# Reordering the front of a fused attention and MLP kernel: first tile's keys and queries first, fewer memsets, memory rows copied on chip, the g product behind the first scores

## Chip, cores and metric

The kernel runs on one core of one Trainium2 chip. The metric is the device time of one execution in microseconds (us). Several executions are timed and the median is quoted. "Fast" runs are those within 1.5% of the fastest run of the same kernel. One execution is also profiled. All times inside an execution are from the start of its span.

## The reference, cut to what matters

Chunked attention is followed by a layer norm and a two-layer MLP with a residual. There are 4 batches of 768 tokens, 8 heads of 64, and d_model is 512.

```python
for c in range(24):                       # chunks of 32 queries
    k_ctx = k[:, :, max(0, 32*c-16) : min(768, 32*c+40)]
    k_full = concat([mem_k, k_ctx]); v_full = concat([mem_v, v_ctx])     # 8 memory rows
    a = softmax(q_c @ k_full.T / 8); out_c = a @ v_full
x  = out.transpose(0, 2, 1, 3).reshape(4, 768, 512)
xn = (x - mean(x)) / sqrt(var(x) + 1e-6) * g_ln
return x + maximum(xn @ w_ch1, 0) @ w_ch2        # 512 -> 2048 -> 512
```

## The kernel before

The work goes by tiles of 128 tokens, and three tiles make a unit (eight units in all). In a unit, `up` runs 16 chunks of 128 hidden columns over the tiles' 384 tokens, then `down` runs three times 16 products. The attention of the next unit is threaded between these. Each engine runs its own list of instructions in order. The front of the program, before the first `up`, has nothing to hide behind, and this change is about it.

```python
def stay_busy(n, p=None):                 # dummies: keep TensorE's clock up (L362-366)
    p = slot("mm") if p is None else p
    for _ in range(n):
        nc.tensor.matmul(out=p, lhsT=busy[:, 0:128], rhs=busy, start=True, stop=True)

def scores(b, t): ...   # L281: 8 matmuls KT x QZ into an att buffer, two exponentials on ScalarE into AT
def values(b, t): ...   # L303: 16 matmuls AT x V into an att buffer
def norm(t, xi): ...    # L315: VectorE; divides by the sums, subtracts the mean, times g_row -> xn
def turn_x(...): ...    # L347: 4 transposes of xn on TensorE, a copy on ScalarE -> xT
def up(u, n, hc, t0=0, on_act=False): ...   # L370: 4 matmuls w1c x xT, then a ReLU into rT
# [cut] first memsets and small loads; then
for h in (0, 4):
    for which in range(2):
        load_kq(0, which, 0, CUT[which], h, h + 4)   # k, q of heads 0-3, then k, q of heads 4-7
make_identity(nc, identity)
stay_busy(10)
clear_v(0, nc.vector, lambda: clear_q(0, 0))         # memsets of V's ones and of QZ, VectorE
clear_q(0, 1); clear_k(0); mem_keys(); mem_cols(0)
stay_busy(4)
v_mem(0)                                             # DMA: memory rows of values into V
for g in range(6): load_v_group(0, g)
# [cut] masks on GpSimd; loads of W1 (load_w1), rest of k and q, W2
banks = [slot("mm")[:, :] for j in range(4)]         # four PSUM banks
first_k = [as16(p) for p in banks]                   # turned keys, pair of heads j in bank j
first = slot("att")
first_q = [as16(first[:, i, :]) for i in range(2)] + first_k[0:2]   # queries j=2,3 share banks 0,1
# [cut] transposes and copies of k, q for j = 0..3
nc.tensor.matmul(out=banks[2], lhsT=ones32, rhs=g_one, start=True, stop=True)   # g to 128 rows
nc.vector.tensor_copy(out=g_row, in_=banks[2])
scores(0, 0); scores(0, 1); stay_busy(3)
values(0, 0); norm(0, 0);   stay_busy(3)
scores(0, 2); values(0, 1); norm(1, 1); stay_busy(1)
turn_x(0, 0, 0, "mm");      stay_busy(3)
values(0, 2); norm(2, 2)
for hc in range(3): up(0, 1, hc, 0, True)            # tile 0 alone
turn_x(0, 1, 1); up(0, 1, 3, 0, True); stay_busy(2)
for hc in range(4): up(0, 2, hc, 1, True)            # tile 1
turn_x(0, 2, 2)
for hc in range(4, 8): up(0, 2, hc)                  # tiles 0 and 1
for hc in range(8): up(0, 3, hc, 2)                  # tile 2
# unit 0 goes on with chunks 8-15 at steps 8-15; beside them:
at(7, clear_q, 1, 0); at(9, clear_q, 1, 1); at(10, clear_k, 1)   # QZ, KT of batch 1
at(15, kq_block, 0, j, 6, NG, ...)                               # "K transposes", tiles 3-5
```

The softmax here doesn't subtract the row's maximum and nothing guards it: scores larger than these inputs give would overflow.

## Time and profile before

| | before |
|---|---|
| time, median of 4 runs beside the changed kernel | 218.57 us (218.41 to 218.89) |
| span of the profiled run | 216.0 us |
| first scores (tile 0) | 12.35 us |
| first values (tile 0) | 14.39 us |
| first `up` | 18.28 us |
| chunk 8 of unit 0 | 24.68 us |
| first K transposes of `kq_block` | 30.71 us |
| last matmul | 212.18 us |

The lines that carry the argument are shown in the prediction below.

### The profile page before, as it was taken

How to read it: one execution, taken by the hardware profiler on the slowest of the kernel's cores; microseconds unless marked ns; L12 is line 12 of the kernel's file. 1: busy time of each engine (PE TensorE's matmuls, PEld its weight loads, DVE VectorE, ACT ScalarE, POOL GpSimd, SP SyncE). 2: the span in 40 equal slices, each digit the busy share in tenths (PEclk: the TensorE clock that was granted, in tenths of full speed). 3: DMA queues.
4: the chain of work that ended last, by engine and by line, in shares of the span. 5: the costliest groups of instructions: out<-in, count | busy, mean ns of one | idle time of the engine just before them, and what ended most of it. 6: DMA issues, size and time to landing. Idle time of an engine off the chain costs nothing.

```text
span 216.0 us, 5059 instructions
## 1 busy us (share of the span) xinstructions
PE 210.2 (97%) x2011; PEld 129.8 (60%) x2011; DVE 118.6 (55%) x274; ACT 99.7 (46%) x206; POOL 104.4 (48%) x185
## 2 busy tenths in 40 slices
PE   7999989999999999999999999999999999999993
PEld 2557866557765577546754676456754675466562
DVE  6967675685737548524375349224484447634222
ACT  4478437855893677302653167103761275314100
POOL 7993245699996318974004998507145000400000
PEclk9999999999999999999999999999999999999998
DMA  5999999999999989996312999997674101330012
GB/s 78 182 150 207 209 208 181 200 206 226 148 140 172 102 135 146 151 146 171 48 27 80 142 186 148 138 156 103 176 150 132 49 3 24 91 108 0 0 49 100
DMA packets 87714, 27.37 MB, mean 127 GB/s; under 512 B 78297, under 2 KB 84185, under 8 KB 87642
## 3 DMA queue, kind: packets, MB, share of 16 engines
q0 software_dynamic: 62128, 14.38, 78.2%
q1 hardware_dynamic: 25562, 12.66, 28.2%
q8 instruction: 16, 0.26, 0.5%
q14 instruction: 8, 0.07, 0.1%
HBM read 28.84 MB, written 6.29 MB: 163 GB/s over the span
## 4 chain that ended last, share of the span: by engine, by line
PE 94%; DVE 3%; ACT 1%; issue 1%; ACTq 0%
PE mm L377 37%; PE mm L394 37%; PE att L289 5%; PE att L309 3%; PE mm L366 3%; PE att L179 2%; PE mm L412 2%; PE mm L179 1%; DVE QZ L436 1%; ACT AT L296 1%; PE att L352 1%; PE att L366 1%; DVE rT L385 1%; PE mm L539 0%; DVE xn L329 0%
## 5 line engine op out<-in xcount | busy, mean ns | idle before, releaser
L377 PE MATMUL mm<-xT,w1c 128*128 128x384 f16 (+2 forms) x560 | 89.0, 313 | 0.6 <-DVE rT L385 0.6
L394 PE MATMUL mm<-w2c,rT 128*128 128x512 f16 x368 | 84.4, 379 | 0.0
L377 PEld LDWEIGHTS <-w1c 128*128 128x128 f16 x560 | 58.8, 114 | 23.6 <-issue 1.0
L383 ACT ACTIVATE rT<-mm 128x384 f16<-128x384 f32 (+2 forms) x74 | 33.1, 453 | 72.4 <-PE mm L377 50.2
L394 PEld LDWEIGHTS <-rT 128*128 128x128 f16 x368 | 34.7, 98 | 37.5
L385 DVE TENSOR_SCALAR rT<-mm 128x384 f16<-128x384 f32 (+2 forms) x66 | 34.9, 533 | 33.6 <-PE mm L377 33.5
L401 DVE SCALAR_TENSOR_TENSOR osb<-mm,rstd,xs 128x512 f32<-128x512 f32 x23 | 17.3, 750 | 41.8 <-PE mm L394 24.9
L296 ACT ACTIVATE AT<-att,band 104x512 f16<-104x512 f32 x48 | 30.2, 683 | 9.6 <-PE att L289 8.2
L338 POOL TENSOR_SCALAR veps<-squares 128x1 f32<-128x1 f32 x24 | 4.8, 200 | 42.7 <-ACT junk L335 41.3
L117 POOL DMA_DIRECT2D V<-in_v_dram x24 | 18.4, 772 | 11.0 <-DMA w1c<-in_moe_w_ch_dram 7.8
L335 ACT ACTIVATE junk<-xs,nmean 128x512 f16<-128x512 f32 x24 | 17.3, 721 | 7.1 <-DVE nmean L326 6.7
L329 DVE SCALAR_TENSOR_TENSOR xn<-xs,nmean,g_row 128x512 f16<-128x512 f32 x24 | 18.8, 782 | 0.9
L320 DVE SCALAR_TENSOR_TENSOR xs<-att,rec 128x512 f32<-128x512 f32 x24 | 16.6, 691 | 0.8
L289 PEld LDWEIGHTS <-KT 128*128 128x128 f16 x192 | 12.6, 98 | 4.6 <-issue 1.0
L277 POOL COPY QZ<-kraw 64x768 f16<-64x768 f16 x16 | 13.2, 826 | 3.9 <-DMA kraw<-qraw 3.4
L342 POOL TENSOR_TENSOR rstd<-veps,mhalf 128x1 f32<-128x1 f32 x24 | 13.7, 571 | 2.0
L289 PE MATMUL att<-QZ,KT 128*128 128x128 f16 x192 | 14.6, 219 | 0.0
L269 POOL COPY KT<-KT 128x128 f16<-128x128 f16 (+4 forms) x16 | 4.2, 292 | 18.2 <-DMA KT<-kraw 18.1
L123 POOL DMA_DIRECT2D V<-in_v_dram x16 | 12.0, 791 | 0.9 <-PE mm L377 0.7
L309 PEld LDWEIGHTS <-AT 104*64 104x64 f16 x384 | 7.5, 111 | 6.5 <-ACT AT L296 2.1
L242 POOL DMA_DIRECT2D qraw<-in_q_dram x12 | 11.3, 938 | 0.0
L242 POOL DMA_DIRECT2D kraw<-in_k_dram x12 | 11.2, 934 | 0.0
(76 smaller groups left out, 136.6 us busy)
## 6 DMA issues: line engine op xcount, KB each, us to landing
out_dram<-osb SPq DMA_DIRECT2D x23, 256.0 KB, 2.3
V<-in_v_dram POOLq DMA_DIRECT2D x36, 96.0 KB, 6.9
w1c<-in_moe_w_ch_dram POOLq DMA_DIRECT2D x4, 512.0 KB, 9.6
w2c<-in_moe_w_ch_dram POOLq DMA_DIRECT2D x4, 512.0 KB, 13.5
kraw<-in_k_dram POOLq DMA_DIRECT2D x12, 128.0 KB, 5.3
qraw<-in_q_dram POOLq DMA_DIRECT2D x12, 128.0 KB, 5.4
qraw<-in_q_dram POOLq DMA_DIRECT2D x3, 384.0 KB, 11.6
kraw<-in_k_dram POOLq DMA_DIRECT2D x3, 256.0 KB, 5.7
```

The source lines that it names most:

```text
L117: nc.gpsimd.dma_start(out=V[b % 2][r : r + hi - lo, g, :, 0:64], in_=dram(v, b * H * HS + lo * D, [[64, hi - lo], [HS, H], [1, 64]]),)
L242: nc.gpsimd.dma_start(out=free(dst, 512 * t, [[64, H], [1, 64]]), in_=dram(src, b * H * HS + 128 * t * D, [[D, 128], [HS, H], [1, 64]]),)
L289: nc.tensor.matmul(out=p[:, gg, 128 * j : 128 * j + 128], lhsT=KT[b % 2][:, (4 * g + j) * KW : (4 * g + j) * KW + 128], rhs=QZ[b % 2][:, g ...
L296: nc.scalar.activation(out=free(a, 32 * c, [[512, 2], [64, 8], [1, 32]], KR), in_=free(p, 32 * c, [[512, 2], [64, 8], [1, 32]], KR), func= ...
L320: nc.vector.scalar_tensor_tensor(out=x.rearrange("p (h d) -> p h d", h=H), in0=free(p, 0, [[128, H], [1, 64]]), scalar=1.0, in1=free(r, 0, ...
L329: nc.vector.scalar_tensor_tensor(out=xn[i], in0=x, scalar=nmean[i], in1=g_row, op0=ALU.add, op1=ALU.mult,)
L335: nc.scalar.activation(out=junk, in_=xs[xi], func=ACTF.Square, bias=nmean[i], accum_out=squares[i],)
L377: nc.tensor.matmul(out=p, lhsT=free(w, i, [[4, 128]]), rhs=xT[u % 2][:, dt, lo:hi], start=(dt == 0), stop=(dt == 3),)
L383: nc.scalar.activation(out=o, in_=p, func=ACTF.Relu)
L385: nc.vector.tensor_scalar(out=o, in0=p, scalar1=0.0, scalar2=None, op0=ALU.max)
L394: nc.tensor.matmul(out=p, lhsT=rT[hc][:, 128 * i : 128 * i + 128], rhs=w2c[hc // 4][:, hc % 4, :], start=(hc == 0), stop=(hc == 15),)
L401: nc.vector.scalar_tensor_tensor(out=o, in0=p, scalar=rstd[t % 9], in1=xs[t % 9], op0=ALU.mult, op1=ALU.add,)
```

## The change

The intent is to reach the first scores sooner. The first tile's groups of keys and queries are evicted before the others. About half of the early memsets are shrunk, moved to ScalarE or put off. The memory rows of V are copied on chip instead of loaded by DMA. The product that spreads g over 128 partitions is issued behind the first scores. With it come a new order of tiles 1 and 2 and a first `up` over two tiles.

```diff
+    def keep_mem(b, g0, g1, copy):          # memv16 -> V[96:104, g0:g1], on an engine
@@ clears
-        eng.memset(V[i][:, :, :, 64:HD], 1.0)
+        eng.memset(V[i].bitcast(FP32)[:, :, :, 32:end], TWO_ONES)     # end = 33 at first
@@ loads
-    for h in (0, 4):
-        for which in range(2):
-            load_kq(0, which, 0, CUT[which], h, h + 4)
+    for which in range(2):
+        load_kq(0, which, 0, CUT[which], 0, 4)
     keep(counts...); make_identity(nc, identity)
+    for which in range(2):
+        load_kq(0, which, 0, CUT[which], 4, H)
+    nc.scalar.copy(out=QZ[0][0:64, 0:6, :, 1, :], in_=<zeros of busy>)
-    clear_v(0, nc.vector, lambda: clear_q(0, 0))
-    clear_q(0, 1)
-    clear_k(0)
+    clear_v(0, nc.vector, lambda: (clear_q(0, 0, 0, 6), clear_k(0)), 33)
-    stay_busy(4)
-    v_mem(0)
-    for g in range(6):
+    for g in range(3):
         load_v_group(0, g)
@@ behind the masks on GpSimd, ahead of W1
+    for g in range(3, 6):
+        load_v_group(0, g)
@@ [cut] K, Q copies of groups 0-1 first; keep_mem(0, 0, 6, vec); then
-    nc.tensor.matmul(out=banks[2], lhsT=ones32, rhs=g_one, start=True, stop=True)
-    nc.vector.tensor_copy(out=g_row, in_=banks[2])
     scores(0, 0)
-    scores(0, 1)
-    stay_busy(3)
+    for j in range(2, 4):
+        for par in range(2):
+            keep_q(on[j], first_q[j], 0, j, par, CUT[1], 2, 6)    # j=2 on ScalarE
+    for i in range(2):
+        nc.tensor.matmul(out=banks[i][:, 256:512], lhsT=ones32, rhs=g_one[:, 256*i : 256*i+256], ...)
+        vec(out=g_row[:, 256*i : 256*i+256], in_=banks[i][:, 256:512])
     values(0, 0); norm(0, 0)
+    stay_busy(1); scores(0, 1); stay_busy(4); values(0, 1); norm(1, 1); scores(0, 2)
+    turn_x(0, 0, 0, "mm"); stay_busy(3); values(0, 2); norm(2, 2); turn_x(0, 1, 1, "mm"); stay_busy(2)
+    # up: chunks 0-3 over tiles 0 and 1, then tile 2; chunks 4-7 over all three
@@ unit 0
-            at(7, clear_q, 1, 0); at(9, clear_q, 1, 1); at(10, clear_k, 1)
+            at(8 + par, clear_q, 0, par, 6, NG)         # par = 0, 1: other half of QZ, batch 0
+            at(11, keep_mem, 0, 6, NG, vec)
+            at(13, <memset of V's other ones>); at(14, <memset of memv16's ones>)
@@ unit 1
+            at(1, clear_q, 1, 0); at(2, clear_q, 1, 1); at(3, clear_k, 1)
```

The lines `values(0, 0)` to `up` are condensed here.

More of the change, by code (lines that the diff above doesn't have):

```diff
@@ L45 @@
     memk16 = sb.tile([128, 2, 64], FP16, name="memk16")
-    memv16 = sb.tile([72, B, H, HD], FP16, name="memv16")[64:72, :, :, :]
-    memv32 = sb.tile([72, 512], FP32, name="memv32")[64:72, :]
+    memv16 = sb.tile([104, B, H, HD], FP16, name="memv16")[96:104, :, :, :]
+    memv32 = sb.tile([104, 512], FP32, name="memv32")[96:104, :]
     memKT = sb.tile([128, B * 4, 8], FP16, name="memKT")
@@ L139, in v_mem @@
                         ap=[list(src.ap[0]), [0, NG], [1, H * HD]]),
+        )
+    def keep_mem(b, g0, g1, copy):
+        src = memv16[:, b, :, 0:64]
+        copy(
+            out=V[b % 2][96:104, g0:g1, :, 0:64],
+            in_=bass.AP(tensor=src.tensor, offset=src.offset,
+                        ap=[list(src.ap[0]), [0, g1 - g0], [HD, H], [1, 64]]),
         )
@@ L432, in clear_k, with clear_q, clear_v @@
         nc.vector.memset(KT[i][:, end : end + 32], 0.0)
-    def clear_q(i, par):
-        nc.vector.memset(QZ[i][64 - 64 * par : 128 - 64 * par, :, :, par, :], 0.0)
-    def clear_v(i, eng, between=lambda: None):
+    def clear_q(i, par, g0=0, g1=NG, eng=nc.vector):
+        eng.memset(QZ[i][64 - 64 * par : 128 - 64 * par, g0:g1, :, par, :], 0.0)
+    TWO_ONES = (2.0 ** -7) * (1 + 15 * 2.0 ** -13)
+    def clear_v(i, eng, between=lambda: None, end=HD // 2):
         eng.memset(V[i][0:32, 0, :, 0:64], 0.0)
         eng.memset(V[i][64:96, NG - 1, :, 0:64], 0.0)
-        eng.memset(V[i][:, :, :, 64:HD], 1.0)
+        eng.memset(V[i].bitcast(FP32)[:, :, :, 32:end], TWO_ONES)
         between()
-        for c, g in enumerate((0, NG - 1)):
+        for c, g, rows in ((0, 0, slice(0, 32)), (1, NG - 1, slice(64, 96))):
             eng.tensor_copy(
-                out=free(V[i][:, g, 0, 64:65], 0, [[HD, H]]),
-                in_=free(counts[:, c : c + 1], 0, [[0, H]]),
+                out=free(V[i][rows, g, 0, 64:65], 0, [[HD, H]]),
+                in_=free(counts[rows, c : c + 1], 0, [[0, H]]),
             )
@@ L462 @@
     nc.vector.memset(mhalf, -0.5)
-    nc.vector.memset(memv16[:, :, :, 64:HD], 1.0)
     nc.sync.dma_start(out=memk32, in_=dram(mem_k, 0, [[64, 128], [128 * 64, 2], [1, 64]]))
@@ L472 @@
     make_identity(nc, identity)
+    for which in range(2):
+        load_kq(0, which, 0, CUT[which], 4, H)
     nc.scalar.copy(out=memk16, in_=memk32)
+    nc.scalar.copy(out=QZ[0][0:64, 0:6, :, 1, :], in_=free(busy[0:64, :], 0, [[0, 6], [0, 4], [1, 64]]))
     nc.scalar.copy(out=memv16[:, 0, :, 0:64], in_=memv32.rearrange("p (h d) -> p h d", h=H))
     stay_busy(10)
-    clear_v(0, nc.vector, lambda: clear_q(0, 0))
-    clear_q(0, 1)
-    clear_k(0)
+    clear_v(0, nc.vector, lambda: (clear_q(0, 0, 0, 6), clear_k(0)), 33)
     mem_keys()
     mem_cols(0)
-    stay_busy(4)
-    v_mem(0)
-    for g in range(6):
+    for g in range(3):
         load_v_group(0, g)
@@ L520 @@
         turn_kq(first_k[j], k16[0], j, CUT[0])
+    stay_busy(2, spare)
     for j in range(2):
@@ L526 @@
             keep_q(act, first_q[j], 0, j, par, CUT[1], 0, 6)
+    keep_mem(0, 0, 6, vec)
     stay_busy(3, spare)
@@ L529 @@
         turn_kq(first_k[j], k16[0], j, CUT[0])
-    for j in range(2, 4):
-        keep_k(first_k[j], 0, j, CUT[0], 0, 7, act if j == 2 else vec)
-    stay_busy(4, spare)
+    stay_busy(2, spare)
     for j in range(2, 4):
         turn_kq(first_q[j], q16[0], j, CUT[1])
-    for g0, g1 in ((0, 2), (2, 6)):
-        for j in range(2, 4):
-            for par in range(2):
-                keep_q(act if j == 2 else vec, first_q[j], 0, j, par, CUT[1], g0, g1)
-    nc.tensor.matmul(out=banks[2], lhsT=ones32, rhs=g_one, start=True, stop=True)
-    nc.vector.tensor_copy(out=g_row, in_=banks[2])
-    scores(0, 0)
-    scores(0, 1)
-    stay_busy(3)
+    on = {2: act, 3: vec}
+    for j in range(2, 4):
+        keep_k(first_k[j], 0, j, CUT[0], 0, 2, on[j])
+    for j in range(2, 4):
+        for par in range(2):
+            keep_q(on[j], first_q[j], 0, j, par, CUT[1], 0, 2)
+    for j in range(2, 4):
+        keep_k(first_k[j], 0, j, CUT[0], 2, 7, on[j])
+    stay_busy(3, spare)
+    scores(0, 0)
+    for j in range(2, 4):
+        for par in range(2):
+            keep_q(on[j], first_q[j], 0, j, par, CUT[1], 2, 6)
+    for i in range(2):
+        nc.tensor.matmul(
+            out=banks[i][:, 256:512], lhsT=ones32, rhs=g_one[:, 256 * i : 256 * i + 256],
+            start=True, stop=True,
+        )
+        vec(out=g_row[:, 256 * i : 256 * i + 256], in_=banks[i][:, 256:512])
     values(0, 0)
     norm(0, 0)
-    stay_busy(3)
-    scores(0, 2)
+    stay_busy(1)
+    scores(0, 1)
+    stay_busy(4)
     values(0, 1)
     norm(1, 1)
-    stay_busy(1)
+    scores(0, 2)
     turn_x(0, 0, 0, "mm")
@@ L554 @@
     norm(2, 2)
-    for hc in range(3):
-        up(0, 1, hc, 0, True)
-    turn_x(0, 1, 1)
-    up(0, 1, 3, 0, True)
+    turn_x(0, 1, 1, "mm")
     stay_busy(2)
+    for hc in range(2):
+        up(0, 2, hc)
+    turn_x(0, 2, 2, "mm")
+    for hc in range(2, 4):
+        up(0, 2, hc)
     for hc in range(4):
-        up(0, 2, hc, 1, True)
-    turn_x(0, 2, 2)
+        up(0, 3, hc, 2)
     for hc in range(4, 8):
-        up(0, 2, hc)
-    for hc in range(8):
-        up(0, 3, hc, 2)
+        up(0, 3, hc)
     units = [[t, t + 1, t + 2] for t in range(0, 6 * B, 3)]
@@ L599 @@
         if u == 0:
-            at(7, clear_q, 1, 0)
-            at(9, clear_q, 1, 1)
-            at(10, clear_k, 1)
+            for par in range(2):
+                at(8 + par, clear_q, 0, par, 6, NG)
+            at(11, keep_mem, 0, 6, NG, vec)
+            at(13, nc.vector.memset, V[0].bitcast(FP32)[:, :, :, 33 : HD // 2], TWO_ONES)
+            at(14, nc.vector.memset, memv16[:, :, :, 64:HD], 1.0)
             at(23, clear_v, 1, nc.gpsimd)
@@ L617 @@
         elif u == 1:
+            at(1, clear_q, 1, 0)
+            at(2, clear_q, 1, 1)
+            at(3, clear_k, 1)
             for j in (0, 2):
```

## The prediction

> **What bounds the kernel now.** I read the busy shares first, then the chain of work that ended last, then that chain cut to the first 45 us, then the timeline of that stretch. The first two are one line each of the page:
>
> ```profile
> PE 210.2 (97%) x2011; PEld 129.8 (60%) x2011; DVE 118.6 (55%) x274; ACT 99.7 (46%) x206; POOL 104.4 (48%) x185
> ...
> PE 94%; DVE 3%; ACT 1%; issue 1%; ACTq 0%
> ```
>
> TensorE (PE) is busy for 97% of the span and owns 94% of the last chain. From 50 to 200 us the table by stretches gives PE 149.97 of 150 us. So whatever is late at 50 us is late at the end: the change is worth exactly what it does to PE in the front, where PE is busy partly with dummies (`stay_busy`, L366). The chain in order of time, cut to the front:
>
> ```profile
> 1.25 4.45 PE mm L366 x10
> ...
> 10.75 0.62 PE mm L179 x32
> 11.37 1.05 PE mm L539 x2
> 12.42 0.57 PE att L289 x8
> ...
> 13.07 1.85 ACT AT L296 x3
> ...
> 18.34 0.79 PE mm L377 x12
> ...
> 25.32 1.34 DVE QZ L436
> ...
> 27.51 1.34 DVE QZ L436
> ```
>
> Columns: start, length, engine and line. The first scores (L289) stand behind the g product (L539, 1.05 us); then come the exponentials (L296); the first useful MLP matmuls (L377) start at 18.3 us. Two clears of QZ for the next batch (L436) sit in the chain at 25.3 and 27.5 us: they delay VectorE's (DVE's) evictions, and PE lost 0.7 us (0.55 of it noted as idle on an eviction) before it went on at 29.31. These are the two things that the change attacks. The timeline of the front has the durations that I use below:
>
> ```profile
> 1.48 0.48 DVE L463 MEMSET memv<- 8x512 f16 x1
> 3.08 1.34 DVE L442 MEMSET V<- 128x1536 f16 x1 [0.38 <-issue]
> 6.52 0.87 SPq L136 DMA_DIRECT2D V<-memv  x1
> 8.73 0.26 DVE L169 COPY KT<-memKT 128x384 f16<-128x384 f16 x1
> 11.16 1.30 ACT L204 COPY QZ<-mm 64x128 f16<-64x128 f16 x4
> 14.39 0.44 PE L309 MATMUL att<-V,AT 104*64 104x65 f16 x16 [0.32 <-ACT AT L296]
> ```
>
> That ACT line is two copies of 64x128 (0.26 each) and two of 64x256 (0.37 each).
>
> **What the Trainium skill says.** (1) "VectorE: DVE Perf Modes", section "Zero memsets can be issued as uint32 (trn2)": a memset takes one cycle per element whatever its type. The trace agrees if the 0.38 us of idle noted ahead of each large one is counted: 1.34 + 0.38 = 1.72 us for 1536 elements. So half of the elements is about 0.85 us, and writing the ones as fp32 pairs halves them too. (2) Same page, section "The perf-mode tier table (the rule you actually need)": a 16-bit copy from SBUF to SBUF can run at four elements per cycle. The only such copy here took 0.26 us (0.40 at worst) for 384 elements, which fits. (3) "SBUF — State Buffer", section "Who interferes with whom": such a copy takes a port pair that GpSimd needs too, and one blocks the other. The spread 0.26 to 0.40 may be that; no run shows it yet. (4) "TensorE: Matmul & The Clock Gate", section "The HAM clock gate (the "warmup" mystery)": the array runs at half clock until it has been busy for some microseconds, and again after an idle window. The dummies show the first half: starts 0.427 us apart at first, 0.216 us from about 6.7 us on.
>
> **The change part by part.**
>
> *Before the first scores.* Four dummies go (1.34 us at half clock). The clears of V and QZ that DVE did before 8.0 us shrink: V ones 1.72 to about 0.16 us, QZ 2 x 1.7 to 0.85, the other half going to ScalarE (ACT). GpSimd makes the identity between the two pairs of k/q loads. The first k load landed at 1.31 + 4.2 = 5.5 us, the first q near 7.05, the second k at 8.44, the second q near 9.5; these come out of one queue that is full from 4 us on, so I leave them. New PE order: k turned at 6.1, q at 7.1, second k at 8.45, second q at 9.5 to 10.0. Copies of the first two groups (0.24 latency + 2 x 0.26) end near 10.7, as do three dummies; scores of tile 0 run 10.65 to 11.1, against 12.35 to 12.95. Gain here: 1.7 us.
>
> *The g product behind the scores.* In the built program the new g matmul (now L561) carries a wait on ACT, and counting ACT's increments it is the last QZ copy out of the same bank (heads j=2, groups 2 to 6). The two touch different columns, but the wait is there. In ACT's order those copies come after both exponentials of tile 0. So: scores end 11.1; exponentials 11.35 to 12.6 (1.27 as now); two copies 0.72, to 13.3; g product 1.05, to 14.4; only then, being in order on PE, the values of tile 0, at 14.4. They start at 14.39 now. **The whole 1.7 us is handed back**, and PE stands idle from 11.1 to 13.3.
>
> *Tiles 1 and 2.* Now both scores are issued before the first values and exponentials 0 and 1 run back to back (four in 2.42 us). In the new order scores(1) follow values(0) and one dummy: 14.95 to 15.4; exponentials 15.6 to 16.9 (now 14.23 to 15.49); values(1) 16.95; scores(2) to 17.7; exponentials 17.95 to 19.2 (now to 17.45); values(2) 19.25; the transpose and copy of tile 1 end at 20.65. The first `up`, which needs two tiles now, starts at 20.7 (one tile at 18.27 now). From there: 4 x 0.436 (256 columns) + 0.22 (turn) + 0.2 (tile 2's xn, DVE, near 21.75) + 4 x 0.22 + 4 x 0.65 = 5.65 us, so chunk 8 starts at 26.35 against 24.65: **+1.7 us**.
>
> *Chunks 8 to 15.* PE needs 8 x 0.65 = 5.2 us. Now it took from 24.65 to 30.70, the stall and small gaps within: about 0.8 is saved. But DVE has there 4 evictions x 0.56, two half clears (1.7), the second copy of mem rows (1.0 by the tier table), the ones of V (672 elements, 0.76) and of memv16 (0.5): 6.2 us. It ends 0.9 late, and the K and Q copies for tile 3 queue behind it, so scores(3) wait about that long. Saved 0.8, lost 0.9: **total +1.8**.
>
> *Unit 1.* Both full clears of QZ (1.7 each) and the K clears (0.7) move to its first steps, where DVE evicts every second chunk (0.56 of every 1.31 us). Four PSUM slots cover about two chunks; I count **+0.6**, like the 0.7 seen now. The DMA for mem rows of batch 0 goes (120 KB, hidden; the loads behind it may come 0.6 us earlier), but W1's first chunk lands at 17.8 us (10.83 + 7.0) and is then needed only at 20.7.
>
> Sum: 1.7 - 0.8 + 0.9 + 0.6 = +2.4 us, so 218.6 + 2.4 = 221.0. Laying out the old program's front with the same durations and waits comes within 0.3 us of its trace.
>
> **The rivals.** *As intended:* the g product runs under exponential 0. Then values(0) start near 12.7; but tile 1's copies still stand behind exponential 0, and its scores behind those: I get `up` at about 19.2 and 219.4 in all. For it speaks that 256 columns of each bank are free; against it, the wait in the program. *DMA as the floor:* even a perfect front can't pass W1's first chunk at 17.8 (17.2 without the mem rows' DMA), with the next every 2.55 us. From there, two tiles' chunks back to back reach chunk 8 at 22.9, and without stall the end is some 2.5 us earlier: 216.1. So faster by over 2% (214.3) is all but excluded. *The clock falls back:* 2.2 us of PE idle in a row, with no dummies to fill it, could bring half clock; the front waits on others for the most part, so perhaps 1 to 2 us more: 222.5. *The copy of mem rows is slow:* at one element per cycle it is 3.2 us instead of 1.0, ahead of tile 0's last copies and again in chunks 8 to 15: some 3 us more, 224. The 0.26 us copy speaks against it, the port that it shares with GpSimd for some of it.
>
> **Range and chances.** 221.0 us. The layout's own error is about 0.7 us; the copy and the clock push upwards, the intended case downwards. Range 219.0 to 223.0 for 8 in 10. Slower by over 2% is above 223.0: chance 0.12, from the last two rivals. Faster: 0.02. Within 2%: 0.86.
>
> **What would show it.** Right: scores of tile 0 before 11.5 us; the g product not before 13 and PE idle ahead of it, released by ACT's QZ copy; values(0) within 0.5 us of 14.4; the first L386 (`up`) after 20 us; no stall in chunks 8 to 15 but one before scores(3); one near the clears in unit 1. Wrong: a g product right behind the scores, a copy of mem rows well over 1.2 us, 512-column dummies 0.43 us apart after 11 us, or PE waiting for W1.

## More of the kernel before

For the comparison that follows, here is the table by stretches of 2 us of the front. Its columns are the stretch, its length, then busy us (and instructions) of TensorE (PE), its weight loads (PEld), VectorE (DVE), ScalarE (ACT) and GpSimd (POOL), then the granted TensorE clock (PEclk, 1.00 is full), the DMA share and GB/s.

```profile
12.00:14.00 2.00, 2.00 (x20) 1.10 (x19) 1.54 (x4) 1.37 (x4) 1.89 (x4) 1.00 3.02 132
14.00:16.00 2.00, 1.68 (x28) 1.07 (x27) 0.99 (x4) 1.49 (x3) 1.96 (x4) 1.00 1.32 201
16.00:18.00 2.00, 1.92 (x33) 0.97 (x32) 1.86 (x7) 1.75 (x3) 0.35 (x1) 1.00 1.24 206
```

TensorE is almost never idle here, and the clock column reads 1.00.

## The result, and the profile after

The changed kernel took 220.97 us (median of 4 runs, 220.08 to 221.73) against 218.57 us. The ratio is 1.0106 (95% interval 1.0058 to 1.0155), which is within 2%. A ratio is the mean time of one kernel's fast runs over the mean of the other's fast runs in the same rounds, so it isn't quite the ratio of the medians.

The page of the changed kernel gives the busy shares, and the last chain by engine:

```profile
PE 210.5 (96%) x1978; PEld 129.6 (59%) x1978; DVE 119.9 (55%) x280; ACT 100.1 (46%) x200; POOL 105.4 (48%) x185
...
PE 86%; DVE 6%; DMA 2%; ACT 2%; issue 1%; POOL 1%; POOLq 0%; DVEq 0%; ACTq 0%
```

TensorE is busy as long as before (210.5 to 210.2 us) with fewer dummies, and it owns 86% of the last chain instead of 94%. The chain in order of time shows who took the rest (start, length, engine and line):

```profile
3.63 4.84 DMA kraw<-in_k_dram
...
11.11 0.46 PE att L298 x8
...
11.66 1.26 ACT AT L305 x2
12.92 0.25 ACT QZ L213
13.18 0.38 ACT QZ L213
...
13.60 1.13 PE mm L561 x4
14.73 0.37 PE att L318 x16
15.10 0.32 PE mm L375
15.42 0.70 PE att L298 x8
16.12 1.71 PE mm L375 x4
...
22.00 1.03 PE mm L386 x8
...
31.27 0.96 DVE V L145
...
38.09 0.44 PE att L298 x5
```

The scores (L298) end near 11.6. Two exponentials follow on ScalarE, then its two QZ copies, and only then the g product (L561) and the values (L318). Four dummies at 16.12 take 1.71 us. Later, VectorE's work of chunks 8 to 15 is on the chain until scores(3), at 38.09. The timeline names the wait and the sizes:

```profile
7.96 0.98 DVE L145 COPY V<-memv 8x3072 f16<-8x3072 f16 x1
8.09 0.90 POOL L502 TENSOR_TENSOR zero<-zero 128x1 f32<-128x1 f32 x1
9.07 0.19 POOL L503 TENSOR_TENSOR band<-band,zero 128x1 f32<-128x1 f32 x1
13.60 1.13 PE L561 MATMUL mm<-g_one,ones 1*128 1x256 f32 x4 [2.04 <-ACT QZ L213]
15.92 1.91 PE L375 MATMUL mm<-busy 128*128 128x512 f16 x4
19.05 0.80 POOL L117 DMA_DIRECT2D V<-in_v_dram  x1 [2.19 <-DMA w1c<-in_moe_w_ch_dram]
```

The bracket at L561 says that TensorE was idle for 2.04 us until ScalarE's copy of QZ. The table by stretches shows what came of it:

```profile
12.00:14.00 2.00, 0.40 (x2) 0.37 (x3) 0.41 (x1) 1.54 (x4) 2.00 (x4) 1.00 1.71 106
14.00:16.00 2.00, 2.00 (x30) 1.48 (x29) 1.63 (x4) 0.00 (x0) 2.00 (x4) 0.86 1.04 148
16.00:18.00 2.00, 2.00 (x16) 0.60 (x13) 0.99 (x4) 1.27 (x2) 0.86 (x2) 0.50 1.22 194
18.00:20.00 2.00, 2.00 (x31) 1.39 (x25) 1.44 (x5) 0.77 (x2) 0.80 (x1) 0.78 1.24 202
```

TensorE is idle for 1.6 of the 2 us from 12 to 14. From about 15.5 to 18.9 us its clock is halved. It looks 100% busy there and does half of the work.

To see where the time went, I cut each trace at five landmarks: first scores, chunk 8 of unit 0, first K transposes, the first `down` product after scores(3) (the ninth of unit 0), last matmul. The lengths in between add up to the last matmul:

| us | first scores | to chunk 8 | to K transposes | past scores(3) | to last matmul | sum |
|---|---|---|---|---|---|---|
| before | 12.35 | 12.32 | 6.03 | 5.03 | 176.45 | 212.18 |
| after | 10.95 | 16.66 | 5.29 | 5.46 | 176.53 | 214.90 |
| difference | -1.40 | +4.34 | -0.74 | +0.43 | +0.08 | +2.72 |

Everything is decided before 38 us. The stretch from the first scores to chunk 8 grew by 4.34 us, and that is what had to be explained.

The four runs of the changed kernel also have a mean granted clock each: 0.992 in the two at 220.08 and 220.34 us, 0.984 in the two at 221.59 and 221.73 us. One stretch of 3.4 us at half clock lowers the mean of a 218 us span by 0.5 x 3.4 / 218 = 0.008. So the slower pair fits two such stretches, or one of twice the length. That is worked out, not seen: only one run has a trace.

### The profile page after: what moved, and what is told of

It reads as the page before. It is cut to its first block, busy times and chain, and to the rows that moved or that the text cites. A ratio compares the mean times of both kernels' runs of the same rounds, so it can differ in the third digit from the quotient of the medians.

```text
span 218.4 us, 4984 instructions
## 1 busy us (share of the span) xinstructions
PE 210.5 (96%) x1978; PEld 129.6 (59%) x1978; DVE 119.9 (55%) x280; ACT 100.1 (46%) x200; POOL 105.4 (48%) x185
## 4 chain that ended last, share of the span: by engine, by line
PE 86%; DVE 6%; DMA 2%; ACT 2%; issue 1%; POOL 1%; POOLq 0%; DVEq 0%; ACTq 0%
PE mm L403 36%; PE mm L386 35%; PE att L298 5%; PE att L318 4%; DMA kraw<-in_k_dram 2%; PE mm L421 2%; PE att L188 1%; DVE rT L394 1%; ACT AT L305 1%; DVE KT L203 1%; PE mm L375 1%; DVE xn L338 1%; DVE xs L329 1%; DVE QZ L445 1%; PE att L361 1%
## 5 line engine op out<-in xcount | busy, mean ns | idle before, releaser
L386 PEld LDWEIGHTS <-w1c 128*128 128x128 f16 x528 | 57.8, 114 | 23.9 <-issue 0.5
L392 ACT ACTIVATE rT<-mm 128x384 f16<-128x384 f32 (+2 forms) x66 | 31.7, 481 | 72.5 <-PE mm L386 51.1
L394 DVE TENSOR_SCALAR rT<-mm 128x384 f16<-128x384 f32 (+2 forms) x66 | 35.4, 540 | 32.5 <-PE mm L386 32.3
L286 POOL COPY QZ<-kraw 64x768 f16<-64x768 f16 x16 | 14.0, 878 | 3.6 <-DMA kraw<-qraw 3.0
L298 PEld LDWEIGHTS <-KT 128*128 128x128 f16 x192 | 13.1, 100 | 4.3 <-issue 0.4
L298 PE MATMUL att<-QZ,KT 128*128 128x128 f16 x192 | 15.4, 223 | 0.3 <-DVE QZ L213 0.3
L351 POOL TENSOR_TENSOR rstd<-veps,mhalf 128x1 f32<-128x1 f32 x24 | 13.3, 553 | 2.0
L318 PEld LDWEIGHTS <-AT 104*64 104x64 f16 x384 | 7.7, 112 | 7.3 <-ACT AT L305 2.7
```

Source lines behind the costliest of these rows:

```text
L298: nc.tensor.matmul(out=p[:, gg, 128 * j : 128 * j + 128], lhsT=KT[b % 2][:, (4 * g + j) * KW : (4 * g + j) * KW + 128], rhs=QZ[b % 2][:, g ...
L386: nc.tensor.matmul(out=p, lhsT=free(w, i, [[4, 128]]), rhs=xT[u % 2][:, dt, lo:hi], start=(dt == 0), stop=(dt == 3),)
L392: nc.scalar.activation(out=o, in_=p, func=ACTF.Relu)
L394: nc.vector.tensor_scalar(out=o, in0=p, scalar1=0.0, scalar2=None, op0=ALU.max)
```

## The experiments

My theory was: (a) the g product's wait for the copies out of its bank hands back the gain; (b) the new order of tiles costs about as much again; (c) the idle time that (a) makes brings half clock on top. Rivals: the copy of memory rows (slower, or in GpSimd's way) is the cause; or the order alone; or W1's arrival. Twelve runs of nine kernels were made (e5, e11 and e12 repeat e2, e10 and e3), all with correct results. In the tables, "after" is the changed kernel. The first four ran on one chip, e5 to e8 on a second, e9 to e12 on a third. Each ratio is against runs of the kernel before beside it. The medians count all timed runs, the ratios only the fast ones: one run of e4 (223.56 us), two of e2 and one of e10 were slow.

| run | what it is | median, us | ratio to before (95%) |
|---|---|---|---|
| e1_fill | after + nine dummies in the gap | 219.26 | 1.0062 (1.0037 to 1.0087) |
| e2_gbank | after, g in other banks | 217.97 | 1.0002 (0.9975 to 1.0030) |
| e3_late_clears | before, clears in unit 1 | 216.72 | 0.9959 (0.9934 to 0.9983) |
| e4_mem_dma | after, memory rows by DMA | 220.06 | 1.0106 (1.0076 to 1.0136) |
| e5_gbank_look | e2 again | 218.63 | 1.0017 (0.9975 to 1.0059) |
| e6_order | e2 + before's order of tiles | 218.64 | 1.0043 (0.9996 to 1.0090) |
| e7_v_first | e6 + V loads together | 217.11 | 0.9957 (0.9921 to 0.9993) |
| e8_late_ones | e7 + ones set later | 216.83 | 0.9946 (0.9905 to 0.9987) |
| e9_kq_first | e8 + k, q loads together | 216.82 | 0.9987 (0.9944 to 1.0030) |
| e10_late_g | e3 + g behind the scores | 217.84 | 0.9999 (0.9973 to 1.0024) |
| e11_late_g_look | e10 again | 218.31 | 1.0007 (0.9974 to 1.0039) |
| e12_clears_again | e3 again | 216.83 | 0.9967 (0.9937 to 0.9998) |

The traces, cut at the same landmarks (the profiled runs of e2 and e10 were disturbed, see there):

| us | first scores | to chunk 8 | to K transposes | past scores(3) | to last matmul | sum |
|---|---|---|---|---|---|---|
| before | 12.35 | 12.32 | 6.03 | 5.03 | 176.45 | 212.18 |
| after | 10.95 | 16.66 | 5.29 | 5.46 | 176.53 | 214.90 |
| e1_fill | 11.23 | 15.68 | 5.29 | 5.47 | 176.50 | 214.17 |
| e3_late_clears | 12.48 | 12.32 | 5.29 | 5.03 | 176.51 | 211.63 |
| e4_mem_dma | 11.53 | 16.66 | 5.29 | 5.03 | 176.48 | 214.99 |
| e5_gbank_look | 10.80 | 14.23 | 5.29 | 5.49 | 176.53 | 212.35 |
| e6_order | 11.04 | 16.25 | 5.29 | 5.61 | 176.52 | 214.71 |
| e7_v_first | 12.10 | 12.97 | 5.29 | 5.46 | 176.48 | 212.31 |
| e8_late_ones | 11.86 | 12.97 | 5.29 | 5.03 | 176.41 | 211.56 |
| e9_kq_first | 11.22 | 12.97 | 5.29 | 5.03 | 176.52 | 211.03 |
| e11_late_g_look | 10.96 | 15.38 | 5.29 | 5.03 | 176.43 | 213.09 |
| e12_clears_again | 12.25 | 12.32 | 5.29 | 5.03 | 176.46 | 211.35 |

### e1_fill: is half clock a part of it?

```diff
     scores(0, 0)
+    stay_busy(9, first[:, 0, :])
```

> The changed kernel with nine 512-column dummies put between the first scores and the g product, into a bank that is free; the wait of the g product stays. Theory (the idle stretch of 2.0 us lets the clock fall): the granted clock stays at 1.00 from 12 to 20 us, the four dummies after scores(1) come 0.216 us apart and not 0.43, values(0) stay at 14.7, the first up comes at 20.7 instead of 22.0, and the time falls by 1.3 us against the fastest runs of the changed kernel: about 218.9 with before at 218.6, and without the spread of 220.1 to 221.7. Rival (the lower clock has another cause, or the front waits on others anyway): clock 0.5 again, or full clock and a time within 0.4 us of 220.1.

Measured: 219.26 us, ratio 1.0062, so 0.44% or 1.0 us of the change's 1.06% is gone (the two intervals overlap a little; the traces are clearer). The table by stretches:

```profile
12.00:14.00 2.00, 1.90 (x10) 0.71 (x8) 0.66 (x2) 1.81 (x4) 2.00 (x4) 1.00 1.67 111
14.00:16.00 2.00, 2.00 (x30) 1.45 (x31) 1.36 (x4) 0.00 (x0) 2.00 (x4) 1.00 1.14 162
16.00:18.00 2.00, 1.51 (x26) 0.74 (x24) 1.28 (x5) 1.26 (x2) 0.79 (x2) 1.00 1.17 178
```

The clock is 1.00 all through, in all six runs, and their spread is 0.54 us instead of 1.65. The stretch from scores to chunk 8 is 15.68 instead of 16.66 us. So useless work in an idle gap made the kernel faster: the half clock costs 0.98 us in the profiled run. It isn't the full 1.7 us that half of 3.4 us would be, because part of it fell into time that would have been waited anyway: the 0.49 us that TensorE waits ahead of values(1) in this trace isn't there in the changed kernel's. The wait for the bank is still there: g starts 2.64 us after the first scores (2.65 in the changed kernel).

### e2_gbank and e5_gbank_look: the wait for the bank

```diff
-            out=banks[i][:, 256:512], lhsT=ones32, rhs=g_one[:, 256 * i : 256 * i + 256],
+            out=banks[2 + i][:, 256:512], lhsT=ones32, rhs=g_one[:, 256 * i : 256 * i + 256],
-        vec(out=g_row[:, 256 * i : 256 * i + 256], in_=banks[i][:, 256:512])
+        vec(out=g_row[:, 256 * i : 256 * i + 256], in_=banks[2 + i][:, 256:512])
```

Banks 2 and 3 held only turned keys, which are copied out before the exponentials.

> The changed kernel with the g product in the upper halves of the two other banks, whose last readers (the K copies) come ahead of the exponentials on ScalarE. Nothing else changes. Theory (the wait on the QZ copies is what hands the front's gain back): g product at 11.7, values(0) at 13.0 instead of 14.7, no idle stretch over 0.6 us, full clock, the first up near 19.3, time 2.5 us below the changed kernel: about 217.8, a little below before. Rival (what costs is that scores(1) stand behind values(0), whatever g does): values(0) at 13.0 all the same but up not before 20.5, and a time of 219.2 or more.

Measured: 217.97 us, ratio 1.0002. The one execution that was profiled took 1,217.92 us and another took 222.88, so its trace couldn't be used, and the same kernel ran again:

> The kernel of e2 once more, for a profile, since the profiled execution of e2 was disturbed (1218 us). Theory: the g product starts at 11.7 to 12.0 and doesn't wait for the QZ copies, values(0) at 13.0 to 13.2, granted clock 1.00 from 12 to 20 us, the first up near 19.4 and the K transposes at the end of unit 0 near 30.3, scores(3) still wait 0.4 us; time within 0.4% of before. If the clock still falls or values(0) stay at 14.7, the reading of e2 is wrong.

Measured: 218.63 us, ratio 1.0017. Its timeline at the g product and the first values:

```profile
11.34 1.12 PE L561 MATMUL mm<-g_one,ones 1*128 1x256 f32 x4
12.83 0.44 PE L318 MATMUL att<-V,AT 104*64 104x65 f16 x16 [0.36 <-ACT AT L305]
```

The g product follows the scores at once and is hidden under the exponentials, and values(0) start at 12.83 instead of 14.66. The changed kernel's loss of 1.06% is gone (0.02% and 0.17% are left). The wait for one bank, with the half clock that came of it, is enough to make the whole loss: an edit of two indices removes both from this trace, and the loss with them. But there is no gain over before either: the stretch from scores to chunk 8 is 14.23 us, still 1.9 longer than before's 12.32, though no clock fell in this front and g costs nothing there. What remains lies behind values(0): from there to chunk 8 it takes 12.21 us, against 10.29 before and 10.28 in e7, which has before's order of tiles again. So it goes with that order.

In this kernel the half clock isn't quite gone: two of the four timed runs have a mean clock of 0.992, two have 1.000.

### e3_late_clears and e12_clears_again: the clears alone

```diff
         if u == 0:
-            at(7, clear_q, 1, 0)
-            at(9, clear_q, 1, 1)
-            at(10, clear_k, 1)
 ...
         elif u == 1:
+            at(1, clear_q, 1, 0)
+            at(2, clear_q, 1, 1)
+            at(3, clear_k, 1)
```

This is done to the kernel before, alone.

> The kernel before with one part alone: the clears of QZ and KT for batch 1 move from steps 7, 9, 10 of unit 0 to steps 1, 2, 3 of unit 1. The prediction's step says that unit 1 then loses 0.6 us and unit 0 gains 0.7 to 0.9: a time within 0.3 us of before. The changed kernel's trace says otherwise (its K transposes of unit 1 keep the distance they had at the end of unit 0: +2.64 and +2.63 us): then the time falls by 0.7 to 0.9 us, to 217.8.

> The kernel of e3_late_clears unchanged, on the chip of e11_late_g_look, to tell whether its gain comes again and to set the two side by side. Expected: ratio 0.995 to 0.998, 0.5 to 0.9 us less than the kernel before, chunk 8 and the later marks 0.6 us earlier. Rival: the 0.9959 of chip 4 was a chance of its runs, and here it is within 0.2% of the kernel before.

Measured: 0.9959 and 0.9967. The stall of 0.74 us in chunks 8 to 15 is gone and nothing comes back later: 176.51 and 176.46 us from `down` to the end, against 176.45. In the second of them the chain in order of time passes through both places without VectorE:

```profile
21.20 8.73 PE mm L377 x80
...
46.69 3.90 PE mm L377 x24
50.59 1.48 PE att L179 x64
```

The first line is chunks 4 to 15 of unit 0 without a break, where the kernel before has its two clears (L436) in the chain. The second is the first six chunks of unit 1, with the first clear beside them; the second clear (50.58 to 51.92 us) runs under the K transposes of the third line. TensorE doesn't wait for either. This part of the change is a gain of 0.3 to 0.4%, and it came twice.

### e4_mem_dma: memory rows by DMA, as before

```diff
-    keep_mem(0, 0, 6, vec)
+    v_mem(0)                                  # ahead of the V loads; ones of memv16 set early
 ...
-            at(11, keep_mem, 0, 6, NG, vec)
-            at(14, nc.vector.memset, memv16[:, :, :, 64:HD], 1.0)
```

> The changed kernel with the mem rows of batch 0 copied by the DMA as before, instead of two copies of 0.97 us on VectorE. Theory: the first copy is hidden (VectorE waits for TensorE after it), the second makes VectorE late at the end of unit 0, where scores(3) wait 0.4 us: that wait goes, the add on GpSimd that took 0.90 us beside the copy takes 0.19 again, and the time falls by 0.4 us at the most, with the clock's spread as it is. Rival (the copies cost what they take): 1.5 us or more less. Rival (the DMA costs more than the copy): slower.

Measured: 220.06 us and a ratio of 1.0106, the same as the change to four digits. The stretch from scores to chunk 8 is 16.66 us in both. The wait before scores(3) is gone (5.03 us), and the first scores came 0.58 us later in its trace; whether the DMA did that or the chance of the run's loads isn't shown. So the copy isn't the cause of the loss, and it isn't a gain either.

### e6_order: before's order of tiles, on top of e2

```diff
     scores(0, 0)
 ...
+    stay_busy(3, first[:, 0, :])
+    scores(0, 1)
     <g product in banks 2, 3>
     values(0, 0); norm(0, 0)
+    scores(0, 2)
+    values(0, 1); norm(1, 1)
+    turn_x(0, 0, 0, "mm"); values(0, 2); norm(2, 2)
+    <up: tile 0 alone, tile 1, both, tile 2, as in the kernel before>
```

The QZ copies of groups 2 and 3 also go ahead of the exponentials, since scores(1) need them, and those of groups 4 and 5 all go to VectorE.

> The kernel of e2 with the order of before from the first scores on: scores(0), scores(1), g product, values(0), scores(2), values(1), values(2), and the first up on one tile as before; the QZ copies are cut so that groups 2 and 3 are there before the exponentials. Theory (what e2 still loses beside its 0.9 us of clears is that scores(1) stand behind values(0) and up waits for two tiles): exponentials 0 and 1 back to back from 11.7 to 14.3, values(2) near 17; the first up then waits for the first chunk of W1, which landed at 19.0 in the changed kernel: time about as e2, 217.7 on a chip where before has 217.7, with the wait on the DMA to be seen. Rival (W1 was late there for another reason and does not bind): first up at 17.5, time 216.5.

Measured: 218.64 us, ratio 1.0043. This was a miss: values(2) start at 17.24 (17.90 in the kernel before), so the order does what it should, but then there is a wait that was hidden until now, and the clock falls after it. The waits of 10 to 30 us (engine and line, what for, us in total, times, longest), and the stretches:

```profile
PE mm L386 <- DMA w1c<-in_moe_w_ch_dram: 1.7, 1, 1.7
```

```profile
18.00:20.00 2.00, 0.58 (x10) 0.59 (x11) 1.75 (x6) 0.13 (x1) 0.34 (x1) 1.00 1.20 195
20.00:22.00 2.00, 2.00 (x17) 1.45 (x16) 0.00 (x0) 1.41 (x5) 0.46 (x1) 0.51 1.24 204
```

W1's first chunk landed only at 19.37 us. Its issue had moved from 10.83 to 11.53 us in the changed kernel, because three V loads were put behind GpSimd's masks and ahead of W1, and are issued from 9.20 us on. The later issue of W1 alone isn't the reason: e4 issued it at 10.79 us and it landed at 18.57, e8 issued it at 11.52 and it landed at 17.06. It goes with the V loads: with three of them late it landed at 18.57 to 19.68 us (changed kernel, e1, e4, e5, e6), with all six together at 16.76 to 17.96 (the seven other traces). In the changed kernel this costs nothing, because its `up` starts at 22.00 anyway.

### e7_v_first: the V loads together again

```diff
-    for g in range(3):
+    for g in range(6):
         load_v_group(0, g)
 ...
-    for g in range(3, 6):
-        load_v_group(0, g)
```

> The kernel of e6 with all six loads of values issued ahead of the constants on GpSimd, as before. Theory (the changed order of GpSimd's issues starved the queue and made W1 1 us late): W1's first chunk lands at 17.2 to 17.8, first up at 17.4 to 18.0, time 1.0 to 1.3 us below e6, 216.5. Rival (W1 does not bind in e6): the same time as e6 within 0.3 us.

Measured: 217.11 us, ratio 0.9957. The wait for W1 is gone and the clock is 1.00; scores to chunk 8 take 12.97 us. (The profiled run was the slowest of its six.) Two things are left: the first scores come late (12.10), and scores(3) wait for VectorE (5.46). This kernel against e6 shows that W1's arrival and the half clock behind it were worth 3.3 us in the traces from scores to chunk 8.

### e8_late_ones: VectorE's backlog ahead of scores(3)

```diff
-            at(13, nc.vector.memset, V[0].bitcast(FP32)[:, :, :, 33 : HD // 2], TWO_ONES)
-            at(14, nc.vector.memset, memv16[:, :, :, 64:HD], 1.0)
+            at(18, nc.vector.memset, V[0].bitcast(FP32)[:, :, :, 33 : HD // 2], TWO_ONES)
+            at(18, nc.vector.memset, memv16[:, :, :, 64:HD], 1.0)
```

> The kernel of e7 with the two memsets of ones (0.62 and 0.48 us on VectorE) moved from steps 13 and 14 of unit 0 to step 18, where VectorE is idle for 3 us. Theory: scores(3) no longer wait for the copies, 0.4 us less than e7, 216.1. Rival (the second copy of mem rows alone makes VectorE late): no change.

Measured: 216.83 us, ratio 0.9946, and 5.03 us past scores(3) instead of 5.46. The wait is gone, so VectorE's backlog made it. TensorE still waits 1.1 us for the second k load:

```profile
9.42 0.69 PE L188 MATMUL mm<-identity,kraw 64*64 64x64 f16 x32 [1.09 <-DMA kraw<-in_k_dram]
```

### e9_kq_first: the first loads of k and q together again

```diff
-    for which in range(2):
-        load_kq(0, which, 0, CUT[which], 0, 4)
+    for h in (0, 4):
+        for which in range(2):
+            load_kq(0, which, 0, CUT[which], h, h + 4)
     keep(counts...); make_identity(nc, identity)
-    for which in range(2):
-        load_kq(0, which, 0, CUT[which], 4, H)
```

> The kernel of e8_late_ones with one thing more: the four loads of the first keys and queries are issued back to back again, as in the kernel before, ahead of the counts and the identity, so this is the changed kernel with its g product, its order of tiles, its V loads and its two memsets of ones mended. In e8_late_ones the second k load landed at 9.38 us (8.44 in the kernel before) and the first scores ran at 11.86. If the place of the identity between the pairs delays those loads, the first scores run near 11.0, the first up near 17.7 to 18.1 (W1's first chunk, landing near 18, is the floor), and the end comes 0.3 to 0.7 us earlier than in e8_late_ones: -0.9 to -1.3 us against the kernel before, ratio 0.994 to 0.996. Rival: the loads land late because the queue is full or by chance of the run, and the first scores stay at 11.8 or so: ratio as in e8_late_ones, or W1 comes later and takes it back.

Measured: 216.82 us. In its trace the second k transposes ran at 8.78 instead of 9.42 us, the first scores at 11.22, the first `up` at 17.79, and the last matmul is 1.15 us earlier than before's. The ratio, 0.9987, is drawn up by one run of 219.53 us at a mean clock of 0.984; the other five lie between 216.35 and 217.91. By the interval it is not shown to be faster than before. That run has no trace; its mean clock fits two stretches of 3.4 us at half clock, so a kernel whose trace shows a full front may still fall now and then.

### e10_late_g and e11_late_g_look: the g product alone, on before

```diff
-    nc.tensor.matmul(out=banks[2], lhsT=ones32, rhs=g_one, start=True, stop=True)
-    nc.vector.tensor_copy(out=g_row, in_=banks[2])
     scores(0, 0)
     scores(0, 1)
+    nc.tensor.matmul(out=banks[2], lhsT=ones32, rhs=g_one, start=True, stop=True)
+    nc.vector.tensor_copy(out=g_row, in_=banks[2])
```

This is on top of e3.

> The kernel of e3_late_clears (the kernel before, with the clears for the next batch in unit 1) with one thing more: the g product is issued behind the scores of tiles 0 and 1, still in its whole bank, which nothing reads by then. This is the change's idea for g alone. If g's 1.05 us ahead of the first scores was on the path, the first scores run near 11.4 and values(0) near 13.5 instead of 14.4, and then W1's first chunk, landing at about 18.1, is the floor of the first up (18.3 before): at most 0.2 us are left of the gain, and the end is -0.6 to -0.8 against the kernel before. Rival: W1 isn't the floor, the front keeps the whole gain: -1.4 to -1.6 us, ratio 0.993.

Measured: 217.84 us, ratio 0.9999. The profiled execution was a disturbed one of 1,221.92 us. Again:

> The kernel of e10_late_g unchanged, because the profiled execution there was a disturbed one (1,222 us, every matmul about six times as long). Its timed runs gave 217.84 us, no gain, where e3_late_clears gave 0.9959. If g's time ahead of the first scores was on the path and W1's first chunk (about 18.1) stops the gain, then here the first scores run near 11.4, values(0) near 13.5, and the first up near 18.2 behind a wait of PE for W1, perhaps with a fall of the granted clock in that wait as in e6_order; the end is -0.6 against the kernel before, or near 0 if the clock falls. Rival: the g product behind the scores delays the values or the evictions by as much as the scores gain, and there is no wait for W1.

Measured: 218.31 us, ratio 1.0007. Neither theory had it whole. The first scores start 1.4 us earlier (10.96), but they wait in pieces for the QZ copies, and the exponentials start at 12.34, only 0.73 us earlier than in the kernel before. There is no wait for W1. And the clock fell, although TensorE was hardly idle:

```profile
11.00:14.00 3.00, 2.37 (x20) 1.26 (x18) 1.58 (x5) 2.73 (x7) 2.90 (x4) 1.00 3.65 115
14.50:17.50 3.00, 3.00 (x24) 1.27 (x23) 1.65 (x6) 0.27 (x1) 1.90 (x4) 0.50 1.27 205
```

So the g product ahead of the scores, in the kernel before, fills time in which the QZ copies are waited for anyway. Moved behind the scores it is no gain by itself (beside its base e12, 0.9967 on the same chip, it is rather slower, though the intervals overlap), and with the small gaps that it leaves the clock fell here.

No version beats before by 2%. The best are the clears alone (e3, e12) and the mended change (e8), at 0.3 to 0.5% less.

## Why the prediction was right or wrong

The time was right: 221.0 predicted, 220.97 measured, and the class with it. The steps were not all right, and two errors cancelled. By the landmarks (predicted, measured, us):

| step | predicted | measured |
|---|---|---|
| first scores | -1.7 | -1.40 |
| waits and order, scores to chunk 8 | +3.4 | +3.36 |
| half clock | 0, named as a rival, "1 to 2 us more" | +0.98 |
| stall in chunks 8 to 15 | -0.8 | -0.74 |
| wait before scores(3) | +0.9 | +0.43 |
| clears in unit 1 | +0.6 | +0.08 |
| sum | +2.4 | +2.7 |

The half clock is read from e1 against the changed kernel (16.66 - 15.68), and waits and order is the rest of that stretch (15.68 - 12.32). The prediction's 3.4 is its 1.7 handed back plus its 1.7 lost by the order. (One slip of a sum: 2% below 218.6 is 214.2, not 214.3; nothing rests on it.)

- **"The whole 1.7 us is handed back": right.** The g product stood idle until ScalarE's last QZ copy, 13.60 us; predicted 13.3. Values(0) came at 14.66; predicted 14.4. The wait was read from the built program, ahead of any run, and e2 and e5 show by one edit that the bank is the cause. The Trainium skill says why it has to be there, in "PSUM — Partial Sum Buffer", section "PSUM bank collisions raise a hardware error": PSUM is to be guarded by bank and quadrant, not by address. The wait for other columns of the same bank agrees with it; no run here let the two collide, and since every bank is one tile of this program, no run tells a guard by bank from one by tile.
- **The order of tiles: right.** Cut once more at values(0), the stretch shows the terms apart. From the first scores to values(0) it takes 2.04 us before, 3.71 in the changed kernel and in e1, and 2.03 in e5, so the bank is worth 1.67. From values(0) to chunk 8 it takes 10.29 before, 11.97 in e1 (no half clock), 12.21 in e5, and 10.28 in e7 with before's order on top. So the order costs 1.7 to 1.9 us, against 1.7 predicted. e7 differs from e5 in the V loads too, but in this stretch of e5 TensorE waits for ScalarE alone, and for no load.
- **The first scores: 0.3 us short.** The loads came as the prediction has them: the second k load landed at 8.47 us, and its transposes ran at 8.52 (predicted 8.45). The step that failed is the stretch behind, "end near 10.7, as do three dummies": from those transposes to the scores the prediction counts 2.2 us, and the trace has 2.43 (8.52 to 10.95), in which TensorE is never idle. Its own list was too long: two groups of transposes and five dummies. "So I leave them" was a risk all the same: with this order of issue the second k load landed at 8.25 to 9.00 us in five traces, but at 9.61 and 9.38 in e7 and e8, where six V loads and not three follow it, and at 8.74 in e9, with the k and q loads together again. How much of that is the order, the V loads or chance of a run stays open.
- **"The clock falls back": a rival that came true.** It was put in the range, not in the number. It cost 0.98 us in the profiled run, and the two slower of the four runs fit twice as long a fall. The prediction had the ingredients (2.2 us of idle TensorE, no dummies to fill it) and should have put about 1 us in the sum.
- **Chunks 8 to 15: right, and scores(3) too large.** VectorE's backlog does hold scores(3) up (gone in e4 and e8, which each take work off it), but by 0.43, not 0.9 us.
- **"+0.6" for unit 1: wrong.** The step that failed is "I count +0.6, like the 0.7 seen now". The same clears that stall TensorE in unit 0 cost nothing in unit 1 (e3, e12: at most 0.06 us). Unit 1 issues K transposes at step 5, so TensorE has work that waits for no ReLU just when VectorE catches up (in e12 the second clear runs under them); I think that this is why, but no run took the transposes away.
- **The copy of memory rows: right in size** (0.98 us, predicted 1.0) and the port rival seen: GpSimd's small add took 0.90 us beside it and 0.19 us just after. In e1, e5 and e6 too the one add of three that fell beside the copy took 0.78 to 0.85 us, and in e4, without the copy, all three took 0.19. It cost GpSimd time, not the kernel.
- **W1: wrong.** "Lands at 17.8 us (10.83 + 7.0)", or 0.6 earlier, keeps the old issue time; it was issued at 11.53 and landed at 18.76. GpSimd's queue waited for it until 19.05 us (18.10 before). Nothing was lost by it here, since `up` came at 22.00, but as soon as the front was mended (e6) it was the next bound.

So the clock (+1.0) made up for the clears and scores(3) (predicted 1.5, measured 0.5). A right total is no proof of right terms.

What stays open: the kernel before varies from 217.1 to 219.3 us from run to run, mostly at a mean clock of 0.997 to 1.000, and no trace here shows why. (A mean of 0.997 needs no fall in the work: in the trace of the kernel before, half clock is recorded from 214.89 us on, behind the last matmul.) The stretch of e11 from scores to chunk 8, 15.38 us, is 3.1 longer than before's, and its trace shows where most of that lies: the scores come in pieces (10.96 to 13.06 us, 2.1 instead of 0.9), then g (1.06), then three dummies, partly at half clock (1.34), so values(0) start 4.50 us after the first scores instead of 2.04.

## What to carry to other kernels

Before moving an instruction earlier or later, list what it will wait for in the new place, by PSUM bank and not by columns: one engine's copy out of a shared bank, queued behind its long operations, can undo the whole move. When a front is full of dummies, an idle gap can cost twice, once as a wait and once as half clock, so fill it with useless work or with something else. And take a new trace after each mended wait: each one here (bank, order, W1, k load) only showed the next.

## What the Trainium skill lacked or had wrong

- "TensorE: Matmul & The Clock Gate", section "The HAM clock gate (the "warmup" mystery)", gives half clock after at least one idle window of about 3.4 us. The length agrees: in all four traces that fall before the last matmul (the changed kernel, e4, e6, e11) the half clock lasts 3.4 us. The condition does not: TensorE was never idle for a whole window. In the 3.4 us ahead of each fall it was idle for about 1.5 us (changed kernel), 1.4 us (e4), 1.7 us (e6) and only 0.6 us (e11). In the three of these other than e6, the g product lies in the same 3.4 us: 1.1 us of matmuls with one row of 128. Counting it as idle gives 1.7 us or more of 3.4 in every fall. Between two changes the clock records of the traces run for whole multiples of 3.41 us (10.24, 13.65, 3.41), and the stretches of that grid without a fall stay just below: 1.66 us in e5 (0.54 idle and g), and 1.72 us idle at the end of the changed kernel, behind its last matmul, against 1.74 in e6. That is a reading that fits these traces by a few hundredths, not one that a run tested by itself. (The page's section "A second HAM failure mode: psum-queue depth-cycling" does tell of short pauses between groups of matmuls that made the clock oscillate, but gives no amount.)
- The same section warns that clock events in a trace can be unreliable. The runs give a case: the disturbed execution of e10 (1,221.92 us), in which ten dummies took 13.30 us instead of 4.45 and the whole span was 5.6 times as long, holds no clock record at all, and `prof` then shows 1.000; what slowed it isn't seen. The first record of the other traces begins at 4.0 to 6.9 us, so the first dummies of every run, 0.43 us apart, are shown at 1.00 too.
- No page that I used has a figure for it: the order of issue in GpSimd's queue moved the landing of a load behind it. W1's first chunk, issued at 10.79 to 11.53 us in all traces, landed at 18.57 to 19.68 us where three of the V loads ahead of it were issued late, and at 16.76 to 17.96 where all six were issued together.
